# Scans of the decays that begin at the inverse of the half products, one copy for the last columns of x, and a planner with a margin on transfers

## The chip, the cores and the metric

The kernel runs on one core of a Trainium2 chip. Its time is the device time of one execution in microseconds (us); the median of three runs counts. Before the change it is 1216.61 us (1216.59 to 1224.62).

## What is computed

Three stages follow each other: a linear attention with decays over 768 steps for 4 x 8 heads of 40 columns, and two dense layers ("MoE" by name) on the 3072 tokens that come out.

```python
# attention: batch 4, heads 8, seq 768, head_dim 40; w in 0.85 to 0.95
for t in range(S):
    y[:, :, t] = einsum('bhd,bhde->bhe', r[t], state)
    Sa = einsum('bhde,bhe->bhd', state, a[t])
    state = state * w[t][:, :, None, :] - outer(Sa, b[t]) + outer(v[t], k[t])
# x: (3072, 320)
h = x @ w_in;  x = (h * cos(h)) @ w_out                      # 320 x 2048, 2048 x 320
h = x @ w_in2; out = (h * clip(h + 3, 0, 6) / 6) @ w_out2
```

## The kernel before

**Tiling.** The sequence is cut into 12 chunks of 64 steps (c); a chunk of one batch entry with its 8 heads is a unit n = 4c + b, 48 in all. Inside a chunk the recurrence is written as matmuls with a unit lower triangular inverse. For it the products of the decays w from the middle of the chunk (after 32 steps) to each step are wanted: forward for steps behind the middle, inverse ahead of it. `decay(g)` makes them for a group of four chunks (g = 0, 1, 2; 128 partitions are 4 chunks x 32 heads): w comes in four pieces of ten columns e, each with 65 values per column of which the first is zero, into `win1` (the tile of the second layer's weights, which is free at the start). For each piece and each direction x a `tensor_tensor_scan` of 650 columns makes running products from 1, restarted at each zero by `one1`; a scaling takes the product at the middle out (`dv`), a reciprocal inverts it (`rc`), and a `tensor_tensor` multiplies the running products with it and turns (e, t) to (t, e) on the way into `wout1`. From there the result goes to DRAM (`Dec`), 32 partitions first for group 0 and the other 96 behind, and `dv` to `D12`. `dsq` squares and sums the result for a range check at the end.

**Steps of a unit.** `pA` loads raw (a, r, b, k) and `pip` (from Dec); `pB` multiplies them and splits them into f16 high and low parts (KBs, ARs); `pT` transposes these by DMA (KBT, ART); `pC` makes the triangular products on PE and masks them (LN, NT); `pL` writes LN to DRAM. For a chunk, `iL` loads it back (Lt), `iB` does 31 steps of the triangular inverse on DVE (each a product into `tmp` and a sum into `Tt`), `iC`, `iC1` write it to DRAM (Tm, Thl) and load it, `iD`, `iE` finish it on PE (`q`). Then `cU`, `cA`, `cAT` (a DMA transpose, FT), `cG`, `cF` make the output and the state of a unit on PE (`t`), `cST` and `cXT` transpose the state and the output (x1T), and copy the last 64 columns of x twice (high and low part), which the first layer's packing of its weights wants.

**Layers.** Weights come as 8-byte floats; `ld_w` loads pieces of 128 x 1024 words and `prep_w` makes f16 high and low parts of them on ACT, DVE and POOL. `mA(m, c, j)` is 16 matmuls of one 512-column piece of layer m for chunk c (two halves in the first chunk), then a sine or a clip on ACT, a product on DVE (`s`) and a split into f16 parts (`ghl`); `mB` multiplies these with w_out (`acc`).

**What sets the order.** Nothing is issued as it is written. Each call is recorded by `Plan.rec` (so nearly all profile lines are L449, the call that emits; L445 is the emission of a copy on ACT) with its dependencies and a cost by a table. `order` then makes a schedule: a list scheduler `forward`, by priorities that `backward` makes from the schedule of the pass before, PASSES times; the instructions stand in the order of the last pass's starts. Ops of `nc.either` are placed on DVE or POOL (copies: DVE or ACT) by the scheduler: POOL takes one where that is not later than `POOL_GAIN` of its cost allows. A DMA, all but two from SP's queue, is counted as queueing behind the ones before it, moving, and then landing 950 ns later. `AHEAD` (hundredths of an op's own duration) and `MARGIN` (times 4 ns) say when an engine is left idle for a more urgent op that will soon be ready. Each engine and SP's queue run strictly in the order made.

Of the kernel before, what the change touches and what calls it, by code (L numbers as in the profile page):

```python
# [10 lines left out]
BF16 = mybir.dt.bfloat16  # L11
# [3 lines left out]
ALU = mybir.AluOpType  # L15
# [4 lines left out]
B, H, S, D = 4, 8, 768, 40  # L20
# [28 lines left out]
SHARE = 20  # L49
SLACK, AHEAD, MARGIN = [0, 0, 0, 0, 0], [0, 20, 0, 0], [0, 50, 20, 0]  # L50
PASSES = 75
RING = {"raw": 2560, "KBT": 2048, "LN": 2048, "v": 1280, "uh": 640, "FT": 2048, "gm": 2048, "pd": 2560, "xy": 1280,
# [28 lines left out]
FULL = (128, 128)  # L81
POOL_GAIN = 0.12
OFFSET = 110
# [3 lines left out]
class Plan:  # L87
# [68 lines left out]
    def rec(self, attr, eng, name, a, kw):  # L156
# [10 lines left out]
        if name.startswith("dma"):  # L167
# [6 lines left out]
            if name == "dma_start":  # L174
                run = _run(outs[0], ins[0])
                run = min(run, 20480)
                dma = by / run * (9 + run * 0.045) / 16
            else:
                r, w = ins[0].shape[0], by // 2 // ins[0].shape[0]
                dma = w / 128 * 204 * r / 128  # L180
                c = 1244.0 if r == 128 and w >= 1024 else 1175.0
# [6 lines left out]
        elif eng in ("DVE", "ANY"):  # L188
            c = 70 + n * 1.042
            es = max(mybir.dt.size(x.dtype) for x in outs + ins)  # L190
            if name == "tensor_copy":
                c = 70 + n * (0.26 if es == 2 else 0.52)
            elif name == "tensor_scalar":
                c = 70 + n * 0.52
            elif name == "reciprocal":
                c = 70 + n * 6.3
            elif name == "tensor_tensor_scan":
                c = 70 + n * 2.08
# [78 lines left out]
    def backward(self, start, pred, users):  # L277
# [4 lines left out]
        on = [engs.index(o["on"]) for o in ops]  # L282
        lat = [LAT.get(o["on"], 0) if o["dma"] is None else 950 for o in ops]
        dur = [o["alt"] if o["alt"] and e > 1 else o["c"] for o, e in zip(ops, on)]
# [54 lines left out]
    def forward(self, pr, pred, users):  # L339
# [51 lines left out]
        while evs:  # L391
# [14 lines left out]
            for e in sorted(touched):  # L406
# [22 lines left out]
                else:  # L429
                    dge = max(dge, t) + 550  # L430
                    dmaf = max(dmaf, dge + 700) + o["dma"]
                    fin = dmaf + 950
                for u in users[i]:
# [59 lines left out]
def kernel(  # L493
# [153 lines left out]
    WQ = EQ * 65  # L647
    one1 = scr_i[:, 2608 + 2 * WQ:2608 + 3 * WQ]
    wslot = [scr_i[:, 652 * k:652 * k + WQ + 1] for k in range(4)]
    wd = [None] * 4  # L650

    def decay_const():
        nc.vector.memset(one1, 0.0)
        nc.vector.memset(one1.rearrange("p (e t) -> p e t", t=65)[:, :, 0:1], 1.0)

    def decay(g):
        o = scr_o[:, 0:2 * C * D]
        ov = o.rearrange("p (t x e) -> p t x e", x=2, e=D)
        z = 4590 + 160 * g
        dv, rc = scr_i[:, z:z + 80], scr_i[:, z + 80:z + 160]  # L660
        for k in range(4):
            (nc.sync, nc.scalar)[k % 2 if g == 0 else 0].dma_start(out=wslot[k], in_=wfwd[g, :, k * WQ:(k + 1) * WQ + 1])
        for k in range(4):
            w = wslot[k]
            es = slice(k * EQ, (k + 1) * EQ)
            for x in range(2):
                q = scr_i[:, 2608 + x * WQ:2608 + (x + 1) * WQ]
                nc.vector.tensor_tensor_scan(out=q, data0=w[:, WQ:0:-1] if x else w[:, 0:WQ], data1=one1, initial=0.0,
                                             op0=ALU.mult, op1=ALU.add)
                qv = q.rearrange("p (e t) -> p e t", t=65)  # L670
                xs = slice(40 * x + k * EQ, 40 * x + (k + 1) * EQ)
                nc.vector.tensor_scalar(out=dv[:, xs], in0=qv[:, ::-1, 32] if x else qv[:, :, 32], scalar1=ISC,
                                        scalar2=None, op0=ALU.mult)
                nc.vector.reciprocal(out=rc[:, xs], in_=dv[:, xs])
                qt = q.rearrange("p (e t) -> p t e", t=65)
                qt = qt[:, C - 1::-1, ::-1] if x else qt[:, 0:C, :]
                nc.either.tensor_tensor(
                    out=ov[:, :, x, es], in0=qt,
                    in1=rc[:, xs].rearrange("p (o e) -> p o e", o=1).to_broadcast([128, C, EQ]), op=ALU.mult)
        cs = slice(g * GRP, (g + 1) * GRP)  # L680
# [11 lines left out]
        for x in range(2):  # L692
            later(T_R if g == 0 else 0.5, dsq, g, x, o)

    def dsq(g, x, o):
        k = COL["dec"][0] + 2 * g + x
        nc.scalar.activation(out=scr_i[:, 2608:2608 + 2 * WQ].bitcast(BF16)[:, 0:C * D],
                             in_=o[:, x * C * D:(x + 1) * C * D], func=AF.Square, accum_out=acc[:, k:k + 1])
# [332 lines left out]
    def cF(n):  # L1031
# [33 lines left out]
        dp("xs", E_XS).tensor_tensor(out=xs[:, 384:704], in0=xy[0:64], in1=xs[:, 0:DM], op=ALU.subtract)  # L1065
        nc.either.tensor_copy(out=xs[:, 320:384], in_=xs[:, 256:320])
        nc.either.tensor_copy(out=xs[:, 704:768], in_=xs[:, 640:704])
        square(xy[0:64], 0, 64, HD, "x", n, xy[0:64])
# [39 lines left out]
    def mB(m, c, j, h=-1):  # L1108
# [15 lines left out]
        for t in ts:  # L1124
            a = ACCS.pop((m, c, t))[:, 0:DM]
            if m == 0:
# [3 lines left out]
                                               op0=ALU.mult, op1=ALU.subtract)  # L1130
                nc.either.tensor_copy(out=xs[:, 320:384], in_=xs[:, 256:320])
                nc.either.tensor_copy(out=xs[:, 704:768], in_=xs[:, 640:704])
                square(xs[:, 0:DM], 0, 128, DM, "o1", 2 * c + t)
# [360 lines left out]
```

## Time and profile before

| | |
|---|---|
| median of three runs | 1216.61 us |
| profiled execution: time, span | 1227.44 us, 1225.7 us |
| busy: PE, DVE, ACT, POOL | 906.8, 1027.2, 805.5, 191.3 us |
| instructions: PE, DVE, ACT, POOL | 11378, 2343, 1727, 213 |
| mean granted TensorE clock | 0.953 |
| bytes moved by DMA | 162.65 MB |

PE is TensorE's matmuls, PEld its weight loads, DVE VectorE, ACT ScalarE, POOL GpSimd, SPq the queue of SyncE, which issues the DMAs. Busy time of an engine counts from an instruction's start to its end; DVE's instructions overlap by some 0.08 us when they are independent. A wait stands on the engine that idles, with what ended it.

### The profile page before, as it was taken

To read this page: it belongs to the slowest core of one execution; us is meant where nothing else is said; L and a number is where in the kernel's file an instruction comes from. 1 tells how busy PE (TensorE), PEld (TensorE's weight loads), DVE (VectorE), ACT (ScalarE), POOL (GpSimd) and SP (SyncE) were. 2 spreads that over 40 slices of the span, in tenths; PEclk is the share of its full clock that TensorE was granted. 3 is DMA by queue.
4 is the path that set the end of the run, shared out by engine and by line. 5 is a ranking of instruction groups with operands and counts; after the bars stand their busy time and mean duration, and the time that the engine had idled before them with its cause. 6 is when DMAs were issued, how large, how long until landed. Compare 5 with 4: busy or idle time off the path is not lost.

```text
span 1225.7 us, 29623 instructions
## 1 busy us (share of the span) xinstructions
PE 906.8 (74%) x11378; PEld 732.4 (60%) x11378; DVE 1027.2 (84%) x2343; ACT 805.5 (66%) x1727; POOL 191.3 (16%) x213
## 2 busy tenths in 40 slices
PE   0000033275798899899998989899889999899994
PEld 0000022274577777687776867777678778688873
DVE  8899999989989979699998978979969869476552
ACT  2654469888779859687786876867857738363241
POOL 3332223323235001021010110100101000000000
PEclk9999999997989989899999989999989989899997
DMA  7978589897887758969888676794865844622010
GB/s 233 215 174 202 169 231 221 160 189 159 130 174 141 143 102 135 172 127 146 125 146 166 108 127 143 126 173 84 143 144 93 127 88 74 92 45 40 1 25 15
DMA packets 474361, 162.65 MB, mean 133 GB/s; under 512 B 446789, under 2 KB 456049, under 8 KB 473826
## 3 DMA queue, kind: packets, MB, share of 16 engines
q1 hardware_dynamic: 473922, 160.00, 66.8%
q8 instruction: 91, 1.49, 0.5%
q14 instruction: 60, 0.49, 0.1%
q10 hardware_dynamic: 288, 0.67, 0.1%
HBM read 80.10 MB, written 25.61 MB: 86 GB/s over the span
## 4 chain that ended last, share of the span: by engine, by line
PE 23%; DVE 17%; DMA 12%; ACT 6%; issue 3%; SPq 3%; DVEq 0%; ACTq 0%
PE h L449 11%; PE acc L449 8%; SPq L449 3%; DVE ghl L449 2%; DVE s L449 2%; DVE Tt L449 2%; DVE tmp L449 2%; PE t L449 2%; PE q L449 2%; DMA pip<-Dec 2%; DMA KBT<-KBs 2%; DVE S8a L449 1%; ACT s L449 1%; DMA Lt<-Tm 1%; DMA x1T<-S8a 1%
## 5 line engine op out<-in xcount | busy, mean ns | idle before, releaser
L449 PE MATMUL acc<-wout,ghl 128*128 128x320 f16 x2304 | 368.7, 307 | 11.7 <-DVE ghl L449 8.6
L449 PEld LDWEIGHTS <-win 128*128 128x128 f16 x3328 | 313.7, 102 | 71.9 <-issue 23.6
L449 PEld LDWEIGHTS <-ghl 128*128 128x128 f16 x2304 | 218.7, 100 | 94.3 <-DVE ghl L449 11.5
L449 ACT ACTIVATE s<-h,cvec 128x512 f32<-128x512 f32 x192 | 130.0, 680 | 134.4 <-PE h L449 91.9
L449 PE MATMUL h<-x1T,win 128*128 128x256 f16 (+1 forms) x1664 | 199.5, 281 | 20.6 <-DVE s L449 13.3
L449 PE MATMUL h<-x2T,win 128*128 128x256 f16 (+1 forms) x1664 | 186.7, 267 | 2.8 <-DVE s L449 2.8
L449 PE MATMUL p<-ART,KBT 120*128 120x64 f16 x384 | 22.0, 207 | 157.5 <-DMA ART<-ARs 64.3
L449 DVE TENSOR_TENSOR ghl<-s,ghl 128x512 f16<-128x512 f32 x190 | 130.8, 689 | 4.8 <-ACT ghl L445 2.7
L449 DVE TENSOR_TENSOR tmp<-Tt,Lt 128x126 f32<-128x126 f32 (+22 forms) x372 | 102.2, 275 | 20.0 <-DMA Lt<-Ls 17.2
L449 PEld LDWEIGHTS <-KBT 120*128 120x128 f16 x384 | 18.5, 106 | 162.8 <-DMA KBT<-KBs 126.9
L449 DVE TENSOR_TENSOR Tt<-Tt,tmp 128x126 f32<-128x126 f32 (+22 forms) x372 | 104.3, 280 | 3.5
L449 DVE SCALAR_TENSOR_TENSOR s<-h,s 128x512 f32<-128x512 f32 x96 | 65.7, 686 | 44.9 <-ACT s L449 44.4
L449 DVE SCALAR_TENSOR_TENSOR s<-s,h 128x512 f32<-128x512 f32 x96 | 64.9, 680 | 30.8 <-ACT s L449 30.3
L445 ACT ACTIVATE ghl<-s 128x512 f16<-128x512 f32 x122 | 75.5, 622 | 22.9 <-DVE s L449 16.7
L449 POOL TENSOR_TENSOR wout<-wout 128x512 int32<-128x512 int32 (+2 forms) x29 | 51.0, 1761 | 118.3 <-ACT wout L449 76.4
L449 PE MATMUL q<-Lt,Tt 32*32 32x32 f32 x768 | 33.3, 204 | 39.3 <-DMA Lt<-Tm 39.0
L449 PE MATMUL t<-E,GF 128*128 128x40 f16 x1152 | 45.2, 183 | 16.6 <-DVE GF L449 12.4
L449 PEld LDWEIGHTS q<-Lt,Tt 32*32 32x32 f32 x768 | 30.5, 119 | 43.8 <-DMA Lt<-Tm 41.1
L449 PEld LDWEIGHTS <-GF 128*128 128x128 f16 x1152 | 38.0, 98 | 22.1 <-DVE GF L449 14.1
L449 PEld LDWEIGHTS <-ART 120*128 120x128 f16 (+1 forms) x704 | 43.5, 105 | 7.7 <-issue 5.1
L449 PE MATMUL t<-FS,NT 128*128 128x40 f16 x768 | 36.6, 183 | 13.9 <-DVE FS L449 5.2
L449 PEld LDWEIGHTS <-NT 128*128 128x128 f16 x768 | 32.2, 98 | 21.7 <-issue 15.6
(158 smaller groups left out, 1742.5 us busy)
## 6 DMA issues: line engine op xcount, KB each, us to landing
raw<-in_arbk_dram SPq DMA_DIRECT2D x46, 320.0 KB
v<-in_vv_dram SPq DMA_DIRECT2D x96, 80.0 KB
pip<-Dec SPq DMA_DIRECT2D x46, 160.0 KB
wout<-in_moe_w_in_dram SPq DMA_DIRECT2D x12, 512.0 KB
Ls<-LN SPq DMA_DIRECT2D x48, 128.0 KB
Lt<-Ls SPq DMA_DIRECT2D x48, 128.0 KB
TT<-Thl SPq DMA_DIRECT2D x12, 512.0 KB
wstat<-in_moe_w_out_dram SPq DMA_DIRECT2D x10, 512.0 KB
```

What stands on the lines that cost most here:

```text
L445: self.nc.scalar.activation(func=AF.Copy, **kw)
L449: getattr(getattr(self.nc, attr), name)(*a, **kw)
```

## The change

In `decay`, the products of both halves of a chunk are made first, by a tree of five multiplies over all 40 columns (32 values to 16, 8, 4, 2, 1); one scaling and one reciprocal for all 80 products follow. The scans then begin at the inverse, which a copy of ten columns puts into `ini`, so that their results need no multiply; a copy turns them to (t, e), and the scans of the second direction run in place. All four pieces of w are needed for the tree. In `cF` and `mB` the two copies of the last 64 columns of x become one. The planner counts a DMA's landing as 1950 ns (LAND), prices scattered `tensor_tensor` and half-height DMA transposes higher, lets the three compute engines hold for urgent ops more often, lets POOL take fewer ops, and makes 46 passes.

```diff
-SLACK, AHEAD, MARGIN = [0, 0, 0, 0, 0], [0, 20, 0, 0], [0, 50, 20, 0]
-PASSES = 75
+SLACK, AHEAD, MARGIN = [0, 0, 0, 0, 0], [100, 100, 200, 0], [20, 20, 20, 0]
+LAND = 1950
+PASSES = 46
...
-POOL_GAIN = 0.12
+POOL_GAIN = -0.03
...
-                dma = w / 128 * 204 * r / 128
+                dma = w / 128 * 204 * (1 if r >= 64 else r / 128)
...
+            elif name == "tensor_tensor" and n > 512 and any(len(x.ap) > 2 and abs(x.ap[-1][0]) > 4 for x in ins):
+                c = 70 + n * 1.906
...
-        lat = [LAT.get(o["on"], 0) if o["dma"] is None else 950 for o in ops]
+        lat = [LAT.get(o["on"], 0) if o["dma"] is None else LAND for o in ops]
...
-                    fin = dmaf + 950
+                    fin = dmaf + LAND
...
-    one1 = scr_i[:, 2608 + 2 * WQ:2608 + 3 * WQ]
-    wslot = [scr_i[:, 652 * k:652 * k + WQ + 1] for k in range(4)]
-    wd = [None] * 4
+    wfl = scr_i[:, 0:4 * WQ + 1]
+    ini = [scr_i[:, 2602 + WQ * x:2602 + WQ * (x + 1)] for x in range(2)]
+    q0 = scr_i[:, 2602 + 2 * WQ:2602 + 3 * WQ]
 
     def decay_const():
-        nc.vector.memset(one1, 0.0)
-        nc.vector.memset(one1.rearrange("p (e t) -> p e t", t=65)[:, :, 0:1], 1.0)
+        for q in ini:
+            nc.gpsimd.memset(q, 0.0)
...
         for k in range(4):
-            (nc.sync, nc.scalar)[k % 2 if g == 0 else 0].dma_start(out=wslot[k], in_=wfwd[g, :, k * WQ:(k + 1) * WQ + 1])
-        for k in range(4):
-            w = wslot[k]
-            es = slice(k * EQ, (k + 1) * EQ)
+            hi = (k + 1) * WQ + (k == 3)
+            (nc.sync, nc.scalar)[k % 2 if g == 0 else 0].dma_start(out=wfl[:, k * WQ:hi], in_=wfwd[g, :, k * WQ:hi])
+
+        v = wfl[:, 0:4 * WQ].rearrange("p (e t) -> p e t", t=65)[:, :, 1:65].rearrange("p e (x t) -> p e x t", x=2)
+        at_, n = 0, 32
+        while n > 1:
+            n //= 2
+            w = o[:, at_:at_ + 2 * D * n].rearrange("p (e x t) -> p e x t", x=2, t=n)
+            nc.vector.tensor_tensor(out=w, in0=v[:, :, :, 0:n], in1=v[:, :, :, n:2 * n], op=ALU.mult)
+            v, at_ = w, at_ + 2 * D * n
+        nc.vector.tensor_scalar(out=dv.rearrange("p (x e) -> p e x", x=2), in0=v[:, :, :, 0], scalar1=ISC, scalar2=None,
+                                op0=ALU.mult)
+        nc.vector.reciprocal(out=rc, in_=dv)
+
+        for k in range(3, -1, -1):
             for x in range(2):
-                q = scr_i[:, 2608 + x * WQ:2608 + (x + 1) * WQ]
-                nc.vector.tensor_tensor_scan(out=q, data0=w[:, WQ:0:-1] if x else w[:, 0:WQ], data1=one1, initial=0.0,
-                                             op0=ALU.mult, op1=ALU.add)
...
-                nc.vector.tensor_scalar(out=dv[:, xs], in0=qv[:, ::-1, 32] if x else qv[:, :, 32], scalar1=ISC,
-                                        scalar2=None, op0=ALU.mult)
-                nc.vector.reciprocal(out=rc[:, xs], in_=dv[:, xs])
...
-                nc.either.tensor_tensor(
-                    out=ov[:, :, x, es], in0=qt,
-                    in1=rc[:, xs].rearrange("p (o e) -> p o e", o=1).to_broadcast([128, C, EQ]), op=ALU.mult)
+                r = rc[:, 40 * x + k * EQ:40 * x + (k + 1) * EQ]
+                nc.either.tensor_copy(out=ini[x].rearrange("p (e t) -> p e t", t=65)[:, :, 0], in_=r[:, ::-1] if x else r)
+                w = wfl[:, k * WQ + x:(k + 1) * WQ + x]
+                q = w if x else q0
+                nc.vector.tensor_tensor_scan(out=q[:, ::-1] if x else q, data0=w[:, ::-1] if x else w, data1=ini[x],
+                                             initial=0.0, op0=ALU.mult, op1=ALU.add)
+                nc.either.tensor_copy(out=ov[:, :, x, k * EQ:(k + 1) * EQ].rearrange("p t e -> p e t"),
+                                      in_=q.rearrange("p (e t) -> p e t", t=65)[:, :, x:C + x])
...
-        nc.either.tensor_copy(out=xs[:, 320:384], in_=xs[:, 256:320])
-        nc.either.tensor_copy(out=xs[:, 704:768], in_=xs[:, 640:704])
+        xv = xs.rearrange("p (x e) -> p x e", x=2)
+        nc.either.tensor_copy(out=xv[:, :, 320:384], in_=xv[:, :, 256:320])
```

In `mB` the copies are changed in the same way.

Orders follow. On DVE, from the program's first loaded data on (win_69 is win1 with the pieces of w, wout_71 is wout1, wout_70 and wstat hold layer weights; a scan prints as SCALAR_TENSOR_TENSOR of 128x650), before:

```order
L449 SCALAR_TENSOR_TENSOR win_69<-win_69 128x650 x2
L449 TENSOR_SCALAR win_69<-win_69 128x10 x2
L449 RECIPROCAL win_69<-win_69 128x10 x2
L449 TENSOR_TENSOR wout_71<-win_69 128x64x10
L449 TENSOR_SCALAR wout_70<-wout_70 128x512
L449 SCALAR_TENSOR_TENSOR win_69<-win_69 128x650
L449 TENSOR_TENSOR wout_71<-win_69 128x64x10
L449 TENSOR_SCALAR win_69<-win_69 128x10
L449 SCALAR_TENSOR_TENSOR wout_70<-wout_70 128x512
L449 SCALAR_TENSOR_TENSOR win_69<-win_69 128x650
L449 RECIPROCAL win_69<-win_69 128x10
```

and now:

```order
L452 TENSOR_TENSOR wout_71<-win_69 128x1280
L452 TENSOR_TENSOR wout_71<-wout_71 128x640
L452 TENSOR_TENSOR wout_71<-wout_71 128x320
L452 TENSOR_TENSOR wout_71<-wout_71 128x160
L452 TENSOR_TENSOR wout_71<-wout_71 128x80
L452 TENSOR_SCALAR win_69<-wout_71 128x40x2
L452 RECIPROCAL win_69<-win_69 128x80
L452 TENSOR_SCALAR wout_70<-wout_70 128x512
L452 SCALAR_TENSOR_TENSOR win_69<-win_69 128x650
L452 COPY wout_71<-win_69 128x10x64
L452 SCALAR_TENSOR_TENSOR win_69<-win_69 128x650 x2
L452 COPY wout_71<-win_69 128x10x64
```

The small scalings and reciprocals are gathered ahead of the scans, and the multiplies of 128x64x10 are gone; two copies of 128x10x64 stand on DVE, the other 22 and all of ten columns on ACT.

On DVE, at the triangular inverse of chunk 0 (`iB`: tmp, then Tt), before:

```order
L449 TENSOR_TENSOR tmp<-Tt,Lt_91 128x110
L449 RECIPROCAL win_69<-win_69 128x10
L449 TENSOR_TENSOR Tt<-Tt,tmp 128x11x10
L449 SCALAR_TENSOR_TENSOR win_69<-win_69 128x650
L449 TENSOR_TENSOR tmp<-Tt,Lt_91 128x108
L449 TENSOR_TENSOR raw_116<-raw_116,pip_80 128x640
L449 TENSOR_TENSOR Tt<-Tt,tmp 128x12x9
L449 TENSOR_SCALAR win_69<-win_69 128x10
L449 TENSOR_TENSOR wout_71<-win_69 128x64x10
L449 TENSOR_TENSOR tmp<-Tt,Lt_91 128x96
L449 TENSOR_TENSOR ARs_78<-raw_116,ARs_78 128x8x40
L449 TENSOR_TENSOR Tt<-Tt,tmp 128x12x8
```

and now:

```order
L452 TENSOR_TENSOR tmp<-Tt,Lt_91 128x120
L452 TENSOR_TENSOR Tt<-Tt,tmp 128x10x12
L452 TENSOR_TENSOR tmp<-Tt,Lt_91 128x121
L452 TENSOR_TENSOR Tt<-Tt,tmp 128x11x11
L452 TENSOR_TENSOR KBs_77<-raw_116,KBs_77 128x8x40
L452 TENSOR_TENSOR tmp<-Tt,Lt_91 128x110
L452 TENSOR_TENSOR Tt<-Tt,tmp 128x11x10
L452 TENSOR_TENSOR tmp<-Tt,Lt_91 128x108
L452 TENSOR_TENSOR Tt<-Tt,tmp 128x12x9
L452 TENSOR_TENSOR tmp<-Tt,Lt_91 128x96
L452 TENSOR_TENSOR Tt<-Tt,tmp 128x12x8
```

The decays of groups 1 and 2 and other work stood between a product and its sum; now, in this piece, each pair stands directly behind each other.

On SP, at the store of group 0's decays (Dec) and the loads that need it (pip, Lt), before:

```order
L449 DMA win_69<-in_wfwd_dram 128x651
L449 DMA wstat<-in_moe_w_in_dram 128x1024
L449 DMA win_69<-in_wfwd_dram 128x651
L449 DMA D_101<-win_69 128x80
L449 DMA Dec_98<-wout_71 32x5120
L449 DMA Dec_98<-wout_71 96x5120
L449 DMA v_136<-in_vv_dram 64x320 x2
L449 DMA wout_70<-in_moe_w_in_dram 128x1024
L449 DMA pip_80<-Dec_98 64x8x80
L449 DMA Lt_92<-Dec_98 64x8x80
```

and now:

```order
L452 DMA win_69<-in_wfwd_dram 128x651
L452 DMA win_69<-in_wfwd_dram 128x650
L452 DMA Dec_98<-wout_71 32x5120
L452 DMA Dec_98<-wout_71 96x5120
L452 DMA wout_70<-in_moe_w_in_dram 128x1024
L452 DMA v_136<-in_vv_dram 64x320 x2
L452 DMA pip_80<-Dec_98 64x8x80
L452 DMA Lt_92<-Dec_98 64x8x80
L452 DMA wstat<-in_moe_w_in_dram 128x1024
L452 DMA win_69<-in_wfwd_dram 128x650
```

A load of layer weights (wstat) that stood ahead of the store now stands behind the loads of the decays; between the store and those loads stand the same three loads as before, in another order.

## Rows read from the trace of the kernel before

**Rows 1.** The page's 40 slices of the span: busy tenths of PE and DVE.

```profile
PE   0000033275798899899998989899889999899994
DVE  8899999989989979699998978979969869476552
```

**Rows 2.** Busy time by stretch: engines, granted clock, DMA share of 16 engines, GB/s.

```profile
core 0: us, PE busy (x) PEld busy (x) DVE busy (x) ACT busy (x) POOL busy (x), PEclk, DMA share, GB/s
0.00:160.00 160.00, 5.31 (x80) 4.45 (x80) 150.08 (x272) 73.39 (x135) 48.94 (x49) 1.00 0.77 197
160.00:240.00 80.00, 23.65 (x448) 20.77 (x448) 77.21 (x180) 68.15 (x147) 23.51 (x25) 1.00 0.90 208
240.00:314.00 74.00, 49.97 (x762) 42.49 (x763) 70.02 (x150) 59.47 (x130) 23.87 (x18) 0.88 0.83 167
314.00:400.00 86.00, 74.64 (x1025) 60.46 (x1024) 77.27 (x170) 72.45 (x157) 31.09 (x28) 0.91 0.83 152
400.00:1208.00 808.00, 753.20 (x9069) 604.26 (x9066) 650.72 (x1568) 531.67 (x1161) 63.92 (x93) 0.96 0.62 110
```

**Rows 3.** Waits of PE between 320 and 1208 us: us in total, times, longest.

```profile
PE p L449 <- DMA KBT<-KBs: 13.8, 6, 3.8
PE q L449 <- DMA Lt<-Tm: 12.1, 5, 3.4
...
PE h L449 <- DMA x1T<-S8a: 7.3, 4, 3.3
PE p L449 <- DMA ART<-ARs: 4.2, 4, 2.2
```

**Rows 4.** Decays on DVE, groups of instructions: busy us, mean ns | idle before.

```profile
L449 DVE TENSOR_TENSOR_SCAN win<-win 128x650 f32<-128x650 f32 x24 | 38.3, 1604 | 3.0 <-DMA win<-in_wfwd_dram 3.0
...
L449 DVE TENSOR_TENSOR wout<-win 128x640 f32<-128x640 f32 x24 | 31.1, 1296 | 0.0
...
L449 DVE TENSOR_SCALAR win<-win 128x10 f32<-128x10 f32 x24 | 4.6, 205 | 0.0
...
L449 DVE RECIPROCAL win<-win 128x10 f32<-128x10 f32 x24 | 4.4, 196 | 0.1
```

**Rows 5.** The nearest operations, groups on DVE and ACT.

```profile
L449 DVE TENSOR_TENSOR raw<-raw,pip 128x640 f32<-128x640 f32 x44 | 36.5, 830 | 2.9 <-DMA raw<-in_arbk_dram 2.8
...
L449 DVE COPY S8a<-Tt 32x256 f32<-32x256 f32 x16 | 6.6, 413 | 0.3
...
L449 DVE TENSOR_TENSOR Tt<-Tt,tmp 128x30 f32<-128x30 f32 x24 | 4.8, 202 | 0.2
...
L445 ACT ACTIVATE KBs<-raw 128x640 f16<-128x640 f32 x35 | 25.4, 726 | 11.5 <-DVE raw L449 11.0 <-DMA KBT<-KBs 0.2
...
L445 ACT ACTIVATE S8a<-S8a 64x64 f16<-64x64 f16 x75 | 18.1, 247 | 7.7 <-DVE S8a L449 7.2
```

**Rows 6.** DVE in order of time: start us, us, instruction; apart and back to back.

```profile
93.57 0.19 DVE L449 TENSOR_TENSOR tmp<-Tt,Lt 128x31 f32<-128x31 f32 x1
93.67 0.68 DVE L449 TENSOR_TENSOR win<-wout,win 128x512 f16<-128x512 f32 x1
...
508.67 0.19 DVE L449 TENSOR_TENSOR tmp<-Tt,Lt 128x31 f32<-128x31 f32 x1 [5.45 <-DMA Lt<-Ls]
508.95 0.19 DVE L449 TENSOR_TENSOR Tt<-Tt,tmp 128x31 f32<-128x31 f32 x1
509.17 0.19 DVE L449 TENSOR_TENSOR tmp<-Tt,Lt 128x30 f32<-128x30 f32 x1
```

**Rows 7.** The first 50 us in order of time, DVE and SP's queue.

```profile
4.84 2.91 DVE L449 TENSOR_TENSOR_SCAN win<-win 128x650 f32<-128x650 f32 x2 [2.99 <-DMA win<-in_wfwd_dram]
...
33.97 0.81 SPq L449 DMA_DIRECT2D Dec<-wout  x2
...
42.66 1.73 SPq L449 DMA_DIRECT2D pip<-Dec  x1
...
50.28 0.81 DVE L449 TENSOR_TENSOR raw<-raw,pip 128x640 f32<-128x640 f32 x1
```

**Rows 8.** DVE and POOL beside each other, in order of time.

```profile
41.91 5.03 DVE L449 TENSOR_TENSOR_SCAN win<-win 128x650 f32<-128x650 f32 x2
...
41.73 1.40 POOL L449 TENSOR_TENSOR wout<-wout 128x512 int32<-128x512 int32 x1 [3.34 <-ACT wout L449]
43.09 2.48 POOL L449 TENSOR_TENSOR wstat<-wstat 128x512 int32<-128x512 int32 x1
```

More of the change, by code (lines that the diff above doesn't have):

```diff
@@ L658, in decay @@
         ov = o.rearrange("p (t x e) -> p t x e", x=2, e=D)
-        z = 4590 + 160 * g
+        z = 4560 + 160 * g
         dv, rc = scr_i[:, z:z + 80], scr_i[:, z + 80:z + 160]
         for k in range(4):
-            (nc.sync, nc.scalar)[k % 2 if g == 0 else 0].dma_start(out=wslot[k], in_=wfwd[g, :, k * WQ:(k + 1) * WQ + 1])
-        for k in range(4):
-            w = wslot[k]
-            es = slice(k * EQ, (k + 1) * EQ)
-            for x in range(2):
-                q = scr_i[:, 2608 + x * WQ:2608 + (x + 1) * WQ]
-                nc.vector.tensor_tensor_scan(out=q, data0=w[:, WQ:0:-1] if x else w[:, 0:WQ], data1=one1, initial=0.0,
-                                             op0=ALU.mult, op1=ALU.add)
-                qv = q.rearrange("p (e t) -> p e t", t=65)
-                xs = slice(40 * x + k * EQ, 40 * x + (k + 1) * EQ)
-                nc.vector.tensor_scalar(out=dv[:, xs], in0=qv[:, ::-1, 32] if x else qv[:, :, 32], scalar1=ISC,
-                                        scalar2=None, op0=ALU.mult)
-                nc.vector.reciprocal(out=rc[:, xs], in_=dv[:, xs])
-                qt = q.rearrange("p (e t) -> p t e", t=65)
-                qt = qt[:, C - 1::-1, ::-1] if x else qt[:, 0:C, :]
-                nc.either.tensor_tensor(
-                    out=ov[:, :, x, es], in0=qt,
-                    in1=rc[:, xs].rearrange("p (o e) -> p o e", o=1).to_broadcast([128, C, EQ]), op=ALU.mult)
@@ L693, in decay @@
             later(T_R if g == 0 else 0.5, dsq, g, x, o)
+    ini_sq = scr_i[:, 0:1280].bitcast(BF16)
     def dsq(g, x, o):
         k = COL["dec"][0] + 2 * g + x
-        nc.scalar.activation(out=scr_i[:, 2608:2608 + 2 * WQ].bitcast(BF16)[:, 0:C * D],
+        nc.scalar.activation(out=ini_sq,
                              in_=o[:, x * C * D:(x + 1) * C * D], func=AF.Square, accum_out=acc[:, k:k + 1])
@@ L1130, in mB @@
                                                op0=ALU.mult, op1=ALU.subtract)
-                nc.either.tensor_copy(out=xs[:, 320:384], in_=xs[:, 256:320])
-                nc.either.tensor_copy(out=xs[:, 704:768], in_=xs[:, 640:704])
+                xv = xs.rearrange("p (x e) -> p x e", x=2)
+                nc.either.tensor_copy(out=xv[:, :, 320:384], in_=xv[:, :, 256:320])
                 square(xs[:, 0:DM], 0, 128, DM, "o1", 2 * c + t)
```

## The prediction

> **What bounds the kernel now.** Read the page's slices first [rows 1]: DVE stands at 8 and 9 from the start to about two thirds of the span, PE at nothing for the first eighth and at 8 and 9 from about slice 10 on. The table of busy time by stretch gives the numbers [rows 2]. In the first 314 us DVE is busy 150.1 + 77.2 + 70.0 = 297.3, so it idles 16.7 us in all, while PE does 78.9 us of work. From 400 on it is the other way round: PE is busy 753.2 of 808 us, DVE 650.7. PE's work is the same before and after the change (the program has the same matmuls), so the time is: when PE becomes full, plus its remaining work, plus what it still idles. I split at 314 us, where PE starts the second unit of the first layer for the second chunk, mA(0, 1, 1). Ahead of it DVE is the limit; behind it PE is, and the 66 us that it idles between 314 and 1208 (86.0 - 74.6 + 808 - 753.2) are the second place where time can go. Of these, waits of matmuls for a landing DMA make 13.8 + 12.1 + 7.3 + 4.2 = 37.4 us, in 19 waits [rows 3].
>
> **The decays, on DVE.** Now three groups of 24 scans, 24 scaled transposing multiplies, 24 small scalings and 24 reciprocals take 38.3 + 31.1 + 4.6 + 4.4 = 78.4 us [rows 4], all of it ahead of the split. After: the 24 scans stay (the same 650 columns; the third operand is another tile of the same shape). Per group five multiplies of 1280, 640, 320, 160 and 80 columns are new. From the rows of 30 columns (0.20 us) and 640 (0.83) [rows 5] one column costs about 1.03 ns, so 1.49 + 0.83 + 0.50 + 0.34 + 0.25 = 3.4 us; with the first one at the price of the strided multiply it would be 2 x 1.30 = 2.6 instead of 1.5, which is the upper bound. One scaling of 80 columns: 0.2 (the row of 10 columns; bound 0.3). One reciprocal of 80 columns: between 0.2, as for 10, and 8 x 0.2 = 1.6; I take the middle, 0.9. Together 4.5 per group, 13.5 for three. Of the 24 transposing copies the order leaves two on DVE; a copy of 256 scattered columns takes 0.41 [rows 5], so 640 lie between 0.41 and 1.03, I take 0.9 each. Sum 38.3 + 13.5 + 1.8 = 53.6: **25 us less on DVE** (bounds 20 to 28).
>
> **What goes to other engines.** 22 copies of 640 columns and all 24 of ten columns go to ACT. The contiguous cast of 640 columns takes 0.73 and the smallest copy 0.25 [rows 5], so 22 x 0.73 + 24 x 0.2 = 21 us. In the first 314 us ACT is busy 73.4 + 68.2 + 59.5 = 201 [rows 2]; 21 more make 222 of 300, so it hides, except the last copy of the first group, which is on the path (counted below). The trace has the scatter only on the read side: 640 columns read at a step of 260 bytes take 1.30 against 0.83 side by side [rows 4, 5]. Where the scattered write is as dear, a copy takes 0.73 x 1.30 / 0.83 = 1.14, 9 us more on ACT, still hidden. The merged copies of x (72 fewer, about 0.2 us each on ACT) save work where ACT has room: nothing.
>
> **A cost on DVE that the order shows.** In the second place shown above, product and sum of the triangular inverse now stand directly behind each other; among the first 600 DVE rows an instruction that reads the result of the one just before it occurs 52 times, against 2 before. Apart, such a product costs the engine 0.10 us (93.57 to 93.67); back to back the next starts 0.22 to 0.28 later (508.67, 508.95, 509.17) [rows 6]. 50 x 0.12 = **6 us more**.
>
> **The first 50 us.** Here not DVE's work but a chain decides: decays, store, load, first product. Now the first scan starts at 4.84, the store of the decays is issued at 33.97, the load of them at 42.66, and the product of raw and decays starts at 50.28, 16.3 after the store [rows 7]. After, the products over halves need all four pieces of w, so I put their start at 6.5 (bounds 5 and 9). Then 4.5 us for the tree, eight scans at 1.5, two copies 1.8, one weight instruction 0.4 and 8 dependent steps at 0.1: 19.5, and 0.73 for the last copy on ACT. The store goes out near 27 instead of 34, and the first product starts near 43: **7 us earlier**. DVE's work ahead of that product falls by more: a third of 25, plus the two scans of the second group that stand there now (41.91, 5.0 us [rows 8]) and come later in the new order, 13 in all. The difference, **6 us**, is idle time that DVE does not have now (bounds 0 and 10).
>
> So the split comes 25 - 6 - 6 = **13 us earlier**. What of the planner's changes is left there (which DVE or POOL op takes a subtraction) moves single microseconds both ways; I count none.
>
> **Behind the split.** The planner now lets a transfer arrive 1 us later than before, so the orders put about 1 us more other work between a DMA and the matmuls that use it. At most that takes 1 us from each of the 19 waits [rows 3], 19 us; at worst the work put in between makes other engines late and nothing is gained, or some is lost. The place of the transfers in SP's queue hardly changes, and a wait that goes often leaves one on DVE behind. I take a third, **6 us less** (bounds -19 and +8). The hold rule (an engine waits for a more urgent op that will be ready within its own duration) shows in no row; it is in that bound.
>
> **Sum.** -25 + 6 + 6 - 6 = -19. The profiled execution took 1227.4 (span 1225.7), 10.8 above the median of the three runs, 1216.6. So 1208 for one like it, and 1216.6 - 19 = **1198 us** as a median.
>
> **Rivals.** *(a) The transfers keep the pace.* The 16 DMA engines are at 0.77, 0.90 and 0.83 in the three stretches ahead of the split [rows 2]. The same transfers in 13 us less need 0.90 x 80 + 0.83 x 74 = 133 us of 141 between 160 and 314. If they can't go faster there, only the 7 us of the beginning stay, and no wait goes: 1216.6 - 7 = 1210. For it: 0.90. Against: DVE, not a DMA, is what ended most of the waits there, since it idles under 7 us in 160 to 314 (77.2 of 80, 70.0 of 74).
>
> *(b) POOL takes it back.* The order gives POOL about 11 us more ahead of the split (memsets of 650 columns, and a few weight subtractions). While POOL worked 1.4 and 2.5 us beside two scans they took 5.03 instead of 2.91 [rows 7, 8], so 0.55 us lost for each of POOL's: 6 us, and 1204. [...]
>
> *(c) Slower: PE's queue is blocked by attention work.* PE runs in order. If the new order puts the 288 small attention groups (six kinds of steps over 48 tiles or 12 chunks) ahead of MoE groups that are ready, and what they need comes late, MoE work stands behind them. The four rows give 37.4 us now; it decides the sign when the groups wait (13 + 6) / 288 = 0.07 us more each than in my sum, and by 0.12 us more each (35 us) the time is 1198 + 35 = 1233. Against it: the margin works the other way.
>
> **How the numbers follow.** A measurement of this kernel tells about 1% from no change: 1204.4 and 1228.8. The forecast, with its own range 1182 to 1204 (all 25 us kept, more waits gone, on one side; half of a rival on the other), 0.62. More than that, below 1182 (no idle, no dependent steps, 12 of 19 us of waits gone), 0.05. (a), 1204 to 1216: 0.13. (b), 1202 to 1210 and so mostly inside 1%: 0.10. Little or nothing gained, up to 1229, 0.02. (c) 0.08. So faster 0.67, same 0.25, slower 0.08. The range 1180 to 1214 leaves out the slow case and small ends on both sides.
>
> **What would show it.** Right: the store of Dec issued near 27, the first raw product near 43, 24 multiplies gone from the lines of DVE and its total near 1005; MoE's first groups and the split ten to fifteen us earlier; the matmuls' waits for KBT, Lt and x1T nearer 30 than 37. Wrong: a store at 30 or later (the copies are dear or block ACT); DVE idle of over 30 us ahead of the split; PE busy share behind it lower than now, with waits on p, q and t; DMA share at 0.95 over 160 to 300.

## The result: 1177.2 us, 41 us less

The median of four runs is **1177.21 us** (1175.69 to 1178.72); the kernel before, in the same comparison, 1218.13 (1216.59 to 1224.62). The ratio is 0.9654, with a 95% interval of 0.9614 to 0.9694: 41 us faster, where 19 were forecast, and below the range. The profiled execution took 1175.7 us, its span is 1173.9, the mean granted clock of TensorE 0.966 (before: 0.953).

The page's slices of the changed kernel, against [rows 1]:

```profile
PE   0010042265997999999999998999999999999994
DVE  7799999979998999799998998988989879676552
```

DVE is as full as before. PE shows one eight and one seven between slice 11 and the last; before it had nine eights and one seven there. Busy time by stretch, against [rows 2] (the columns are the same):

```profile
0.00:160.00 160.00, 15.81 (x260) 13.64 (x260) 139.53 (x245) 105.58 (x193) 43.67 (x59) 1.00 0.85 211
160.00:240.00 80.00, 21.41 (x417) 19.14 (x416) 78.18 (x176) 66.44 (x139) 25.50 (x19) 1.00 0.92 204
240.00:314.00 74.00, 49.62 (x670) 41.47 (x670) 66.18 (x152) 62.18 (x136) 28.13 (x23) 0.82 0.82 163
314.00:400.00 86.00, 74.87 (x1043) 60.87 (x1041) 81.25 (x174) 73.36 (x155) 31.24 (x27) 0.92 0.75 160
400.00:1158.00 758.00, 729.90 (x8998) 591.92 (x8996) 642.35 (x1533) 516.84 (x1082) 72.28 (x98) 0.98 0.64 114
```

From 400 on PE now idles 28 us of 758; before it was 55 of 808. And PE's own work became shorter: with the same 11378 matmuls it is busy 891.6 us in all, before 906.8. The split, the first matmul of mA(0, 1, 1), stands at 311.6; before at 313.6. So 2 of the 52 us between the two profiled executions lie ahead of the split, and all the rest behind it.

PE's waits between 320 and 1158, against [rows 3] (us in total, times, longest):

```profile
PE h L452 <- DVE s L452: 6.9, 10, 2.1
PE acc L452 <- DVE xs L452: 6.8, 3, 4.3
PE q L452 <- DMA Lt<-Tm: 5.7, 4, 2.0
PE t L452 <- DVE GF L452: 5.5, 7, 2.2
PE p L452 <- DMA KBT<-KBs: 3.3, 3, 1.6
PE t L452 <- DMA FT<-FS: 2.3, 1, 2.3
...
PE q L452 <- DMA raw<-in_arbk_dram: 0.9, 1, 0.9
```

Waits for transfers are 5.7 + 3.3 + 2.3 + 0.9 = 12.2 us, a third of the 37.4 of before; x1T and ART are gone from the list.

The decays in the first 320 us of the changed kernel, DVE and then ACT (busy us, mean ns | idle before), against [rows 4]:

```profile
L452 DVE TENSOR_TENSOR_SCAN win<-win 128x650 f32<-128x650 f32 x24 | 36.9, 1548 | 1.1 <-ACT wout L448 0.9
L452 DVE TENSOR_TENSOR wout<-win 128x1280 f32<-128x1280 f32 x3 | 4.5, 1488 | 5.8 <-DMA win<-in_wfwd_dram 5.8
L452 DVE TENSOR_TENSOR wout<-wout 128x640 f32<-128x640 f32 x3 | 2.5, 819 | 0.0
L452 DVE RECIPROCAL win<-win 128x80 f32<-128x80 f32 x3 | 1.9, 647 | 0.0
L452 DVE COPY wout<-win 128x640 f32<-128x640 f32 x2 | 1.4, 719 | 0.1
```

```profile
L448 ACT ACTIVATE wout<-win 128x640 f32<-128x640 f32 x22 | 28.2, 1289 | 1.6 <-DVE win L452 1.4
L448 ACT ACTIVATE win<-win 128x10 f32<-128x10 f32 x24 | 4.5, 211 | 9.8 <-DVE win L452 9.8
```

And its first 50 us, in order of time, against [rows 7]:

```profile
6.94 1.49 DVE L452 TENSOR_TENSOR wout<-win 128x1280 f32<-128x1280 f32 x1 [5.83 <-DMA win<-in_wfwd_dram]
...
26.99 0.80 SPq L452 DMA_DIRECT2D Dec<-wout  x2
...
35.01 2.24 SPq L452 DMA_DIRECT2D pip<-Dec  x1
...
44.17 0.83 DVE L452 TENSOR_TENSOR raw<-raw,pip 128x640 f32<-128x640 f32 x1 [0.47 <-ACT pip L448]
```

### The profile page after: what moved, and what is told of

It is laid out like the page before. It is cut to its first block, busy times and chain, and to the rows that moved or that the text cites. A ratio compares the mean times of both kernels' runs of the same rounds, so it can differ in the third digit from the quotient of the medians.

```text
span 1173.9 us, 29549 instructions
## 1 busy us (share of the span) xinstructions
PE 891.6 (76%) x11378; PEld 727.0 (62%) x11378; DVE 1009.4 (86%) x2282; ACT 824.4 (70%) x1701; POOL 200.8 (17%) x225
## 5 line engine op out<-in xcount | busy, mean ns | idle before, releaser
L452 PE MATMUL acc<-wout,ghl 128*128 128x320 f16 x2304 | 361.0, 304 | 11.7 <-DVE xs L452 6.8
L452 PEld LDWEIGHTS <-win 128*128 128x128 f16 x3328 | 309.6, 101 | 55.4 <-issue 14.8
L452 PE MATMUL h<-x1T,win 128*128 128x256 f16 (+1 forms) x1664 | 194.1, 276 | 10.8 <-DVE s L452 10.4
L452 DVE TENSOR_TENSOR ghl<-s,ghl 128x512 f16<-128x512 f32 x185 | 128.2, 693 | 5.0 <-ACT ghl L448 2.6
L452 POOL TENSOR_TENSOR wout<-wout 128x512 int32<-128x512 int32 (+2 forms) x30 | 47.9, 1600 | 102.6 <-ACT wout L452 46.0
L452 PEld LDWEIGHTS <-ART 120*64 120x64 f16 (+1 forms) x704 | 43.1, 105 | 14.3 <-issue 10.6
L452 ACT ACTIVATE wout<-wout 128x512 f32<-128x512 f32 (+3 forms) x56 | 37.0, 662 | 15.6 <-DMA wout<-in_moe_w_in_dram 11.3
L452 POOL TENSOR_TENSOR wstat<-wstat 128x512 int32<-128x512 int32 (+1 forms) x16 | 30.4, 1898 | 102.5 <-ACT wstat L452 80.4
```

What stands on the lines that cost most here:

```text
L452: getattr(getattr(self.nc, attr), name)(*a, **kw)
```

## The experiments

Theories on record with the first runs: A, the prediction (DVE's work ahead of the split); B, the margin on transfers makes the gain behind it; C, any other order moves the time by 10 us or more, and the gain is such a draw. D to H came as the runs did; each text says what it means. Differences below are against the kernel before, run beside each on the same chip (its median lay between 1218.1 and 1221.4).

**One part at a time.** `e1_body` is the changed kernel with the planner of before (all of its numbers and costs); `e2_planner` is the kernel before with the new planner; `e3_land` changes only the landing time in the kernel before; `e4_noland` takes only that out of the changed one.

```diff
# e3_land: before +
-        lat = [LAT.get(o["on"], 0) if o["dma"] is None else 950 for o in ops]
+        lat = [LAT.get(o["on"], 0) if o["dma"] is None else 1950 for o in ops]
-                    fin = dmaf + 950
+                    fin = dmaf + 1950
# e4_noland: after +
-LAND = 1950
+LAND = 950
```

> Only the new decays and the merged copies, planned by the planner of before (landing 950 ns, its old hold rule, costs, POOL rule and 75 passes). Theory A (the prediction): the 25 us of DVE work gone ahead of the split give 13 us, so 1205 us against 1218. Theory B (the margin on transfers makes the gain behind the split): the body alone gives under 5 us, 1213 to 1223. Theory C (any new schedule of the same rules moves the time by 10 us or more, and the gain is such a draw): anywhere from 1195 to 1230, without a relation to DVE's work.

> The kernel of before with the whole new planner (landing 1950 ns, hold rule, POOL rule, costs, 46 passes) and the old decays and copies. Theory A: the planner alone gives 6 us, 1212. Theory B: it gives most of the 41 us, 1177 to 1187, with waits of matmuls for DMAs behind 320 us near 12 us instead of 37. Theory C: somewhere between 1180 and 1220, with the waits not following.

> The kernel of before with one number changed: a transfer is planned to land 1950 ns after it moved instead of 950. Theory A: 1212. Theory B: 1185 to 1195, and the matmuls' waits for KBT, Lt, x1T and ART behind 320 us fall from 37 us to 15 or less. Theory C: within 10 us of 1218 on either side.

> The changed kernel with the landing planned at 950 ns again, the rest as changed. Theory A: 1183 (6 us slower than 1177). Theory B: 1205 to 1220, the waits for DMAs back at 30 us or more. Theory C: within 10 us of 1177.

Measured: `e1_body` 1204.3 us (-17, ratio 0.9872, 0.9817 to 0.9927), `e2_planner` 1209.5 (-12, 0.9919, 0.9885 to 0.9952), `e3_land` 1227.6 (+6, 1.0037, 1.0005 to 1.0069), `e4_noland` 1211.7 (-10, 0.9922, 0.9897 to 0.9947). The size of `e1_body` fits A, its place does not: its split stands at 313.7, as before, and the whole gain lies behind it. `e2_planner` is near A's 1212, but A missed the other two (1212 and 1183). B falls in its simple form: the margin alone gains nothing, though the changed kernel without it loses 34, as B said. PE's waits behind 314 us show what the margin did, the rows for DVE in the kernel before and the first rows of `e3_land`:

```profile
PE h L449 <- DVE s L449: 9.3, 9, 2.5
PE t L449 <- DVE GF L449: 3.5, 6, 0.9
```

```profile
PE h L449 <- DVE s L449: 15.1, 11, 5.1
PE t L449 <- DVE GF L449: 9.1, 7, 4.0
PE q L449 <- DMA Lt<-Tm: 6.2, 4, 3.6
```

In `e3_land` all waits for transfers are 15.4 us (before 37.8), but those for DVE 43.4 (before 24.8), and the split came at 331.4. The changed kernel without the margin has the opposite first row:

```profile
PE q L452 <- DMA Lt<-Tm: 21.6, 5, 8.7
```

**Other orders of the same kernels.** A different number of passes makes another order out of the same costs.

```diff
# c1_b76, c2_b46: before +
-PASSES = 75
+PASSES = 76 (46)
# c3_a47, c4_a75: after +
-PASSES = 46
+PASSES = 47 (75)
```

> The kernel before with one more pass of its planner (76 for 75), nothing else: another order from the same costs. Theory C (every other order moves the time by 10 us or more, and the 41 us are in good part such a draw): over 10 us away from 1221, to either side. Theory D (what the first runs left: the margin on transfers takes 18 us out of the part behind mA(0, 1, 1), the decays 25 there or 13 ahead of it, and both add up): 1211 to 1231, with PE's waits for DMAs behind 314 us at 30 us or more and the split between 310 and 320.

> The kernel before with 46 passes for 75, the number of the changed kernel. C: over 10 us away from 1221 to either side, and away from the order of 76 passes as well. D: 1211 to 1231, PE's waits for DMAs behind 314 us at 30 us or more.

> The changed kernel with 47 passes for 46. C: over 10 us slower than 1177, since 46 passes was then a lucky order; 1190 or more. D: 1170 to 1187, PE's waits for DMAs behind the split at 10 to 18 us.

> The changed kernel with 75 passes for 46, the number of the kernel before. C: over 10 us slower than 1177. D: 1170 to 1187, PE's waits for DMAs behind the split at 10 to 18 us.

Measured: `c1_b76` 1226.0 (+5, 1.0042, 1.0013 to 1.0070), `c2_b46` 1230.8 (+10, 1.0090, 1.0054 to 1.0127), `c3_a47` 1191.4 (-29, 0.9750, 0.9701 to 0.9799), `c4_a75` 1186.0 (-35, 0.9714, 0.9665 to 0.9764). Three orders of each kernel: 0, +5, +10 and -41, -29, -35 against the kernel before, so +5 and -35 in the mean. C falls as the cause: the means lie 40 us apart. But the six orders lie up to 7 us to either side of their means; `c3_a47` was outside what D had given it and where C had put it (1190 or more), `c2_b46` is at C's limit of 10 us, and the waits for transfers of `c1_b76` and `c2_b46` (29 us) are a little under D's 30, those of `c4_a75` (9) under its 10. Each kernel as it stands is the best of its three, so some luck is in both times; their difference, 41, is still about that of the means.

**Price of DVE's time, of bytes, and of the margin's size.**

```diff
# x1_dve: after +, the first multiply over halves of groups 1 and 2 ten times
+            for _ in range(10 if g and n == 16 else 1):
                 nc.vector.tensor_tensor(out=w, in0=v[:, :, :, 0:n], ...)
# x2_dma: after +, the pieces of w of groups 1 and 2 loaded three times
+            for _ in range(3 if g else 1):
                 (nc.sync, nc.scalar)[...].dma_start(out=wfl[:, k * WQ:hi], ...)
# x3_l1450, x4_l2450: after +
-LAND = 1950
+LAND = 1450 (2450)
```

> The changed kernel in which the first multiply over halves of the second and third group is done ten times instead of once: 18 x 1.49 = 27 us more on DVE ahead of the split, about what the change saved there. Theory D (DVE's time ahead of the split counts in full, though it shows only behind it): the orders of the changed kernel lie at 1177 to 1191, so 1204 to 1218. Theory E (transfers set the pace ahead of the split, so DVE's time is free there and the gain is the margin's alone): 1177 to 1195. At the split, mA(0, 1, 1): D 320 or later, E 312 to 318.

> The changed kernel in which the pieces of w of the second and third group are loaded three times instead of once: 16 loads of 325 KB more, 5.2 MB, about 26 us of all queues at the 200 GB/s that the stretches ahead of the split show. E: 20 us or more slower than 1185, so 1205 or more, the split at 330. D: 1177 to 1195, the split at 312 to 320, since 0.85 to 0.92 of DMA share leaves room for a part and DVE is what is waited for.

> The changed kernel with a margin of 1450 ns for 1950: half of what the change added. With 950 it was 1212. D (the margin takes PE's waits for DMAs away, 37 us at 950 and 12 at 1950, and each us of them counts more than once by the clock): between, 1190 to 1200, waits for DMAs behind 314 us about 22. Theory C (draws of orders alone): no trend, anywhere between 1177 and 1212.

> The changed kernel with a margin of 2450 ns for 1950. D: what is left of waits for DMAs is 12 us, so little more to gain, and the start-up, in which nothing lies between a transfer and its user, pays: 1175 to 1190, waits for DMAs at 5 to 10 us. C: 1177 to 1212 without a trend.

Measured: `x1_dve` 1209.4 (-10, 0.9935, 0.9900 to 0.9971), `x2_dma` 1210.6 (-9, 0.9916, 0.9881 to 0.9951), `x3_l1450` 1188.6 (-31, 0.9722, 0.9658 to 0.9785), `x4_l2450` 1191.1 (-29, 0.9744, 0.9685 to 0.9802). Against the -35 of the changed kernel's orders, 27 us more on DVE cost 25, as D said, with the split at 337. (Each of these is one order, so such a cost is known to some 7 us.) The row of DVE's multiplies there, and for the loads the row of issues of `x2_dma` (count, KB each):

```profile
L452 DVE TENSOR_TENSOR wout<-win 128x1280 f32<-128x1280 f32 x21 | 31.9, 1519 | 6.0 <-DMA win<-in_wfwd_dram 5.9
```

```profile
win<-in_wfwd_dram SPq DMA_DIRECT2D x20, 325.0 KB
win<-in_wfwd_dram SPq DMA_DIRECT2D x6, 325.5 KB
```

The 5.2 MB more cost 26 us as well, as E said, though its split came at 319.6 and not at 330. So D and E were no alternatives: each addition was paid nearly in full. Whether in `x2_dma` it is the bytes, the sixteen issues in SP's queue, or the later start of the decays that costs, was not separated. The gain does not grow in proportion to the margin: at 950, 1450, 1950 and 2450 ns the difference is -10, -31, -41 and -29, and PE's waits for transfers behind 314 us are 37.3, 13.9, 12.2 and 9.5 us. D had 22 for 1450; half of the margin already takes nearly all of the waits. In time the last three can't be told apart, since they lie within the spread of orders; `x4_l2450` came out just above D's 1175 to 1190.

**Second orders of the halves, and what was left.** `y1` to `y4` repeat `e1`, `e4`, `e2` and `e3` with another number of passes. `y5_nohold` takes out of the changed kernel only the rule for holding back, `y6_copies` only the merged copies.

```diff
# y1_body76: e1_body with PASSES = 76      # y2_noland47: e4_noland with PASSES = 47
# y3_planner47: e2_planner with PASSES = 47   # y4_land46: e3_land with PASSES = 46
# y5_nohold: after +
-SLACK, AHEAD, MARGIN = [0, 0, 0, 0, 0], [100, 100, 200, 0], [20, 20, 20, 0]
+SLACK, AHEAD, MARGIN = [0, 0, 0, 0, 0], [0, 20, 0, 0], [0, 50, 20, 0]
# y6_copies: after + (in both places)
-        nc.either.tensor_copy(out=xv[:, :, 320:384], in_=xv[:, :, 256:320])
+        nc.either.tensor_copy(out=xs[:, 320:384], in_=xs[:, 256:320])
+        nc.either.tensor_copy(out=xs[:, 704:768], in_=xs[:, 640:704])
```

> New decays and copies, the planner of before, 76 passes: a second order of run e1. Theory D (the parts add up: decays and copies about 17 to 32, planner 12 to 27): 1197 to 1211. Theory F (neither does anything without the other, and 1204 was a lucky order): 1215 or more.

> The changed kernel with the margin back at 950 ns and 47 passes: a second order of run e4. D: 1204 to 1218, PE's waits for DMAs behind 314 us at 30 us or more. F: 1204 to 1218 as well. If the loss of run e4 was that order alone: under 1195.

> The old decays and copies with the whole new planner, 47 passes: a second order of run e2. D: 1199 to 1214. F: 1215 or more.

> The kernel before with the margin at 1950 ns and 46 passes: a second order of run e3. D (the margin takes 15 to 20 us out of the part behind the split whatever stands ahead of it): 1205 to 1217, so run e3 was an unlucky order. F (without the time that the decays free on DVE, the margin only moves the waits from DMAs to DVE and puts the split later): 1220 or more, waits for DMAs at 15 us and for DVE at over 35.

> The changed kernel with the rule for holding back as before. Its three orders lie at 1177 to 1191, mean 1185. Theory G (with the decays and the margin in place, holding back is worth the 10 to 18 us that lie between runs e3 and e2, or y1 and y2): 1195 or more. Theory H (decays and margin make the gain): 1177 to 1191.

> The changed kernel with the two copies of the last columns of x apart again, 72 instructions of about 0.2 us more on ACT and DVE. The prediction had them at nothing: 1177 to 1191. If they stand on DVE while it is the limit, up to 72 x 0.2 = 14 us: 1195 or more.

Measured: `y1_body76` 1223.8 (+6, 1.0028, 0.9994 to 1.0061), `y2_noland47` 1196.4 (-22, 0.9806, 0.9735 to 0.9877), `y3_planner47` 1208.2 (-10, 0.9907, 0.9875 to 0.9940), `y4_land46` 1226.0 (+8, 1.0052, 1.0018 to 1.0085), `y5_nohold` 1209.3 (-11, 0.9912, 0.9875 to 0.9948), `y6_copies` 1193.4 (-27, 0.9776, 0.9726 to 0.9825). `y1` contradicts D's reading of `e1` and is what F said: the decays alone are worth little in this order, 23 us less than in that of `e1`, so their worth without the planner stays uncertain. `y2` came out 8 us faster than either theory had it; the margin's share is then smaller than `e4` said. `y3` agrees with D and not with F, `y4` with F in the time; its waits for transfers are 24.5 us, not 15, those for DVE 37.6. `y5` is G's: the rule for holding back, for which the prediction had no term, is worth as much as the others, by one order. PE's first waits without it, from 320 us on:

```profile
PE h L452 <- DVE s L452: 14.5, 12, 2.3
PE q L452 <- DMA Lt<-Tm: 10.8, 6, 3.9
PE t L452 <- DVE GF L452: 7.8, 7, 4.1
```

`y6` lies 8 us above the mean of the three orders and 2 above the slowest of them: one order does not tell that from nothing.

**All kernels in one table.** Split: start of mA(0, 1, 1). Idle: PE's idle time from there to its last matmul. Clock: an estimate of what PE lost to a granted clock under 1 behind 316 us, the sum over stretches of 4 us (my choice) of busy time times one minus the granted clock. Waits: PE's behind 314 us, for transfers and for DVE. All in us, of one profiled execution each; the difference is that of the medians. The profiled execution of the kernel before ran 9 us above its median and that of y5 7 above, those of e2 and y2 8 and 7 below; the others lie within 3.5 of theirs.

| kernel | difference | split | idle | clock | for DMA | for DVE |
|---|---|---|---|---|---|---|
| before; c1; c2 | 0; +5; +10 | 314; 321; 319 | 66; 69; 71 | 34; 23; 30 | 38; 29; 29 | 25; 30; 33 |
| margin alone: e3; y4 | +6; +8 | 331; 331 | 57; 65 | 33; 30 | 15; 25 | 43; 38 |
| decays, copies: e1; y1 | -17; +6 | 314; 319 | 56; 64 | 20; 27 | 27; 33 | 22; 29 |
| planner: e2; y3 | -12; -10 | 325; 325 | 46; 49 | 20; 21 | 15; 16 | 29; 29 |
| after, no margin: e4; y2 | -10; -22 | 314; 316 | 67; 45 | 17; 18 | 37; 24 | 22; 18 |
| after, old holding: y5 | -11 | 320 | 60 | 33 | 18 | 36 |
| after; c3; c4 | -41; -29; -35 | 312; 318; 314 | 39; 50; 44 | 17; 15; 20 | 12; 13; 9 | 24; 36; 31 |

Means over the orders, against the +5 of the kernel before: margin alone +2, decays and copies -11, planner -16, all -40. Taken out of the whole, the margin costs 19, the decays with the copies 24, the rule for holding back 24 (one order). These sum to 67, more than the whole, so the parts need each other: the margin without freed time on DVE and without holding back only turned waits for transfers into waits for DVE. The planner's new rule for POOL and its two new prices were never taken out or put in by themselves.

## Why the prediction was wrong, step by step

**DVE's work: right.** The decays were to fall from 78.4 to 53.6 us. They fell to about 51: scans 36.9, the two largest multiplies 4.5 + 2.5, the three small ones and the scaling about 4, reciprocals 1.9, two copies 1.4. The reciprocal was between its ends (0.65, taken 0.9). DVE's total went from 1027.2 to 1009.4, 18 less; about 1005 was the sign given. Over three orders of each kernel it is 22 less.

**ACT: dearer.** The 22 scattering copies take 28.2 us, 1.29 each, above the 1.14 that was the upper end, and the 24 small ones 4.5. These copies write 4 bytes at a time, 320 bytes apart; a cast of as many columns side by side takes ACT 0.73 [rows 5]. On DVE the same copy takes 0.72, a cast of as many columns side by side 0.49 and a multiply 0.83 [rows 5], so the scatter costs less there, if it costs anything. No run tells what makes it dearer on ACT, nor what the dearer copies cost the kernel.

**The first 50 us: right.** Store of Dec at 26.99 (forecast near 27), first product at 44.17 (near 43). DVE idles 13.9 us of these 50, before 6.8: 7 more, where 6 were forecast.

**The split 13 us earlier: wrong for the change, and only in part right for the decays.** Over the orders the split moved by 3 us only (317.7 to 314.6). With the old planner the new decays hardly move it: it stands at 314 and 319 in `e1` and `y1`, at 314, 321 and 319 in the orders of the kernel before. With the new planner they do: from 325 in both `e2` and `y3` to 312, 318 and 314, 10 us in the mean. The pair of orders in which the 13 come out is `y3_planner47` (324.6) and the changed kernel (311.6). Busy time up to the split, first the one, then the other:

```profile
0.00:325.00 325.00, 82.54 (x1284) 72.36 (x1285) 307.52 (x615) 198.83 (x406) 88.35 (x88) 0.95 0.82 187
```

```profile
0.00:312.00 312.00, 84.84 (x1324) 72.59 (x1325) 281.89 (x567) 232.25 (x462) 97.30 (x100) 0.96 0.86 198
```

DVE is busy 25.6 us less and idles 12.6 more, which looks like the -25 and the 6 + 6 of the prediction. That is partly luck. The first six is there (the first 50 us). The second, for steps that follow each other directly, does not show: products and sums of the inverse (tmp, Tt) take 206.5 us of DVE before and 208.5 after. What idles instead, behind the first load, are mostly waits for ACT: up to the split 7, 10 and 7 us in the orders of the kernel before, 17, 16 and 13 in those of the changed kernel. In the two longest ACT had itself waited for a load of weights, first DVE's row, then ACT's:

```profile
42.15 0.43 DVE L452 TENSOR_SCALAR wout<-wout 128x512 int32<-128x512 int32 x1 [3.25 <-ACT wout L452]
245.24 0.42 DVE L452 TENSOR_SCALAR wout<-wout 64x512 int32<-64x512 int32 x1 [2.81 <-ACT wout L452]
```

```profile
41.36 0.66 ACT L452 ACTIVATE wout<-wout 128x512 f32<-128x512 f32 x1 [6.00 <-DMA wout<-in_moe_w_in_dram]
244.45 0.67 ACT L452 ACTIVATE wout<-wout 64x512 f32<-64x512 f32 x1 [3.49 <-DMA wout<-in_moe_w_in_dram]
```

With the old planner nearly all of DVE's freed time became idle time: up to the split it is busy 281 and 282 us and idles 32 and 37 in `e1` and `y1`, where the orders of the kernel before have 297 to 302 and 17 to 19. What failed for the whole change is the sentence "I count none" on what the planner's changes do ahead of the split. In both orders of `e2` and `y3` they put it 4 to 11 us later than in the three of the kernel before, the margin alone 10 to 18; with the margin alone DVE is busy 313 us up to it, so other work was put first. The split was also a poor mark: in `e2` and `y3` that unit stands one place earlier among the units of its chunk, and in `y6_copies` it starts at 334, with 94 us of PE's work ahead of it instead of 84, and the time is near that of the others.

**Behind the split, 6 us less with an end of 19: the step that failed.** Means over three orders each: idle time from 68.6 to 44.1, busy time from 822.4 to 807.7, together **39 us**. Three things were mis-sized.
- The waits for transfers fell from 37.8 to 12.2 us, 26 and not 6 (over three orders from 32 to 11). The margin did not take 1 us from each of 19 waits; most of them went altogether (20 to 9).
- I looked for the holding rule in the rows of waits and, finding none, gave it no term of its own. The 66 us of idle time were the place, not the 37 that wait for transfers. All kernels with the new rule but `e4` (67) and `x2` (55) stand at 39 to 50 us of idle, those without it at 56 to 71.
- "PE's work is the same" was true of the matmuls and false of their time. The clock's column is 34, 23 and 30 before, 17, 15 and 20 after: 11 us in the mean. It goes with the idle time only roughly (`e4` lost 17 with 67 us of idle, `e3` 33 with 57), and in the rows that follow the lower clock comes behind a wait. In the kernel before, PE waits 2.26 us for KBT, and its rows of 4 us (busy, granted clock, DMA share, GB/s) go on so:

```profile
565.39 0.60 PE L449 MATMUL p<-ART,KBT 120*128 120x64 f16 x8 [2.26 <-DMA KBT<-KBs]
```

```profile
560.00:564.00 4.00, 3.13 (x27) 1.00 1.08 116
564.00:568.00 4.00, 2.61 (x17) 0.68 0.97 218
568.00:572.00 4.00, 4.00 (x31) 0.89 0.84 141
572.00:576.00 4.00, 4.00 (x54) 1.00 0.82 174
```

One of the waits of the changed kernel shows it too:

```profile
375.52 3.36 PE L452 MATMUL acc<-wout,ghl 128*128 128x320 f16 x12 [4.33 <-DVE xs L452]
```

```profile
368.00:372.00 4.00, 3.00 (x64) 1.00 0.72 135
372.00:376.00 4.00, 0.48 (x2) 0.82 0.88 152
376.00:380.00 4.00, 4.00 (x23) 0.50 0.35 52
380.00:384.00 4.00, 4.00 (x53) 0.83 0.34 51
384.00:388.00 4.00, 4.00 (x75) 1.00 0.51 87
```

After the wait PE's granted clock is 0.50 in a whole row and 0.83 in the next: by the estimate of the table 2.0 and 0.7 us lost, on top of the 4.33. The matmuls agree: the twelve of acc behind the wait take 3.36 us, the twelve at 379.12 us 2.90, and twelve at 386.74, with the clock at 1.00, 1.79, so 2.7 us more for the first two groups. What sets the clock was not shown: the wait of 1.12 us that ends at 368.19 has a row at 1.00 behind it. The sum for the part behind the split is then 25 of idle and 15 of busy time, of which 11 are the clock by that estimate and 3 are work that PE had done ahead of the split.

**The rivals.** (a), transfers that keep the pace: the split hardly moved, as it said, but 27 us of DVE's time put back cost 25, so DVE's time was not free; in part it was right, since more loads cost as well (26 us in `x2_dma`) and some of DVE's freed time ended in waits behind a load. (b) did not come: POOL is busy 97.3 us up to 314 instead of 96.3, and the scans got no slower (1.55 us each, before 1.60). (c) went the other way: the attention groups wait less (for KBT 3.3 us instead of 13.8, for Lt 5.7 instead of 12.1). The merged copies, costed at nothing, remain undecided between 0 and 8 us. The range of (b) goes up to 1210, as if all of POOL's 11 us were lost to DVE; no run shows that. Its rows [rows 7, 8] have 0.55 us of two scans lost for each us of POOL's `tensor_tensor` beside them, and for the two memsets of 650 columns, 1.2 us in all, no loss is shown.

**What stays open.** How the 40 us divide among the parts: each is known only with one to three orders, which differ by up to 14 us (`e1` and `y1` by 23), and the POOL rule and the two prices have no run of their own. And why holding back and the margin help each other is argued from the waits, not shown by a run of its own.

## What to carry to other kernels

Where one engine bounds a stretch, count all of its idle time there as what a better order can win (here 66 us), not only the waits that a row names (37), and look in the rows behind a wait for what a lower granted clock adds (here 2.7 us behind one of 4.33). A change of a planner's numbers can't be costed by the waits it aims at, since a wait that goes may come back on another engine (in `e3_land` those for transfers fell from 37.8 to 15.4 us, those for DVE rose from 24.8 to 43.4); its parts are best tested by taking each out of the whole, with at least two orders. And a time freed on one engine ahead of the place where another becomes the bound need not move that place (in `e1` and `y1` DVE was busy 15 to 21 us less up to the split, which stood at 314 and 319, in the three orders of the kernel before at 314 to 321).

## What was not expected of the hardware

- The same scattering copy of 640 columns takes 1.29 us on ACT and 0.72 on DVE, while side by side, in a cast to f16, ACT takes 0.73 and DVE 0.49.
- The same 11378 matmuls are busy between 884.1 us (`x4_l2450`, granted clock 0.969) and 907.5 (`y5_nohold`, 0.951).
- A reciprocal of 80 columns takes 0.65 us, one of ten 0.20 [rows 4]: about 6 ns for each column more, an estimate from these two, where a multiply of 640 takes 1.3 ns a column with everything in it (0.82 us).
